# Reordering the first-token turns of a gated SSM and MLP kernel, turning the last of them into one PSUM bank, and taking a small exponential ahead of two copies

## Chip, cores and metric

One NeuronCore of a Trainium2 chip (trn2) runs the program. The metric is the device time of one execution in microseconds (us). "Fast" runs are those not marked as disturbed. A ratio of two kernels is the mean time of one kernel's fast runs over the mean of the other's in the same rounds, so it is not quite the ratio of the medians that are quoted beside it. "Span" is the length of one execution inside the profile; it is about 1.8 us shorter than the time.

## The reference

`x` has 2048 tokens of 640 channels. The output mixes a linear state-space layer `a` and a two-layer GELU network `b`:

```python
g = sigmoid((x * gate_w).sum(-1, keepdims=True))
# a: h_t = Lam_bar * h_{t-1} + B_bar x_t  (complex, 640 states), y = 2 Re(C h) + x * Dskip
#    with dt = exp(log_dt), Lam_bar = exp(dt * Lam)
# b: gelu(x @ w1 + b1) @ w2 + b2,  w1 is 640 x 1728
return g * a + (1 - g) * b
```

The recurrence is real once the complex rotation is taken out with tables of sine and cosine. The tables and the decay `r_c = exp(dt * Re(Lam))` come from three small parameter vectors.

## The kernel before

Tokens go in four chunks of 512. Matmuls want `x` with channels on the partitions. Later chunks are transposed by DMA, but the first chunk is "turned" by TensorE: a matmul of a 128 x 128 piece of `x` with the identity, into PSUM, then a copy from PSUM to `xT`. There are four token tiles (0 to 3) and five channel blocks (0 to 4). Blocks 0 and 1 of a tile are turned first (`turn_first`), blocks 2 to 4 later (`turn_rest`), because their half of `x` lands later.

Between the turns TensorE already works on the first layer. `part(kd, a)` is six matmuls of 128 columns: channel block `kd` of token tile `a`, into six accumulators, one PSUM bank each.

```python
KA = 2                                   # blocks 0, 1 first; 2, 3, 4 are "the rest"
def turned(engine, p, col, a, k0, k1):   # PSUM -> xT, on VectorE or ScalarE
    dst = xT[0][:, k0:k1, a * P:(a + 1) * P]
    src = p[:, col:col + (k1 - k0) * P].rearrange("p (k t) -> p k t", t=P)
    ...
def turn_first(a, other):
    t = bank()
    turn(t, 0, a, 0);          turned(nc.vector, t, 0, a, 0, 1)
    turn(other, a * P, a, 1);  turned(nc.scalar, other, a * P, a, 1, 2)
# [cut]
def turn_rest(a, parts):
    for k0, k1, t, engine in parts:
        for k in range(k0, k1):
            turn(t, (k - k0) * P, a, k)
        turned(engine, t, 0, a, k0, k1)

part(0, 0); part(0, 1)                   # [one call a line in the source]
turn_first(2, pA)
part(1, 0)
turn_first(3, pA)
part(1, 1)
part(0, 2)
turn_rest(0, ((KA, KD, bank(), nc.scalar),))
part(1, 2)
# parameters: turned into pA, copied to colA, then dt16 = exp(log_dt) and limp
part(0, 3)
turn_rest(1, ((KA, KD, bank(), nc.vector),))
part(1, 3)
turn_rest(2, ((KA, KD, pA, nc.scalar),))
part(2, 0)
nc.vector.tensor_tensor(out=dtl[:], in0=dt16[:], in1=lre_c, op=ALU.mult)      # the two products
nc.vector.tensor_tensor(out=thp_c[:], in0=dt16[:], in1=limp[:], op=ALU.mult)
turn_rest(3, ((KA, KA + 1, bank(), nc.vector), (KA + 1, KD, pA, nc.scalar)))
nc.scalar.activation(out=r_c[:], in_=dtl[:], func=ACT.Exp)                    # the decay
# sine and cosine tables from thp_c [cut]
part(2, 1); part(2, 2); part(2, 3)
```

The kernel's PSUM pool holds eight banks. Six are the accumulators and one is the fixed bank `pA`. That leaves **one** for every `bank()` call in this stretch: I call it the rotating bank. A turn into either bank must wait until the copy that last read it has finished.

Of the kernel before, what the change touches and what calls it, by code (L numbers as in the profile page):

```python
# [16 lines left out]
P = 128  # L17
# [5 lines left out]
KD = D // P  # L23
# [18 lines left out]
def kernel(  # L42
# [19 lines left out]
    nc = tc.nc  # L62
# [12 lines left out]
    def bank(dtype=F32):  # L75
        return ps.tile([P, CH * 4 // (4 if dtype == F32 else 2)], dtype, name="bank")
# [55 lines left out]
    KA = 2  # L132
# [95 lines left out]
    pA = bank()  # L228
# [3 lines left out]
    def turn(p, col, a, kd):  # L232
        nc.tensor.matmul(p[:, col:col + P], lhsT=xn[0][:, a, kd * P:(kd + 1) * P], rhs=ident[:], start=True, stop=True,  # L233
                         skip_group_check=True)

    def turned(engine, p, col, a, k0, k1):
        dst = xT[0][:, k0:k1, a * P:(a + 1) * P]
        src = p[:, col:col + (k1 - k0) * P].rearrange("p (k t) -> p k t", t=P)
        if engine is nc.vector:
            nc.vector.tensor_copy(out=dst, in_=src)  # L240
        else:
            nc.scalar.activation(out=dst, in_=src, func=ACT.Identity)  # L242

    def turn_first(a, other):
        t = bank()
        turn(t, 0, a, 0)
        turned(nc.vector, t, 0, a, 0, 1)
        turn(other, a * P, a, 1)
        turned(nc.scalar, other, a * P, a, 1, 2)
# [76 lines left out]
    def strip(kd, t0, t1, first, f0=0, f1=FA):  # L326
        for kf in range(f0, f1):
            ff1_mm(banks[kf], 0, kf, kd, t0, t1, first, 3)

    def turn_rest(a, parts):  # L330
        for k0, k1, t, engine in parts:
            for k in range(k0, k1):
                turn(t, (k - k0) * P, a, k)
            turned(engine, t, 0, a, k0, k1)

    HB = CH // 2

# [18 lines left out]
    def over(c, n):  # L356
        return c.rearrange("p (k o) -> p k o", o=1).to_broadcast([P, KS, n])

    def part(kd, a):
        strip(kd, a * P, (a + 1) * P, kd == 0)  # L360
# [2 lines left out]
    part(0, 1)  # L363
    turn_first(2, pA)
    part(1, 0)
    turn_first(3, pA)
    part(1, 1)
    part(0, 2)
    turn_rest(0, ((KA, KD, bank(), nc.scalar),))
    part(1, 2)  # L370
    nc.tensor.matmul(pA[:, 0:3 * KS], lhsT=prmA[:], rhs=ident[:, 0:3 * KS], start=True, stop=True, skip_group_check=True)  # L371
    nc.vector.tensor_copy(out=colA[:], in_=pA[:, 0:3 * KS])
    nc.scalar.activation(out=dt16[:], in_=ldt_c, func=ACT.Exp)
    nc.vector.tensor_scalar(out=limp[:], in0=lim_c, scalar1=INV_2PI, scalar2=None, op0=ALU.mult)
    part(0, 3)
    turn_rest(1, ((KA, KD, bank(), nc.vector),))
    part(1, 3)
    turn_rest(2, ((KA, KD, pA, nc.scalar),))
    part(2, 0)
    nc.vector.tensor_tensor(out=dtl[:], in0=dt16[:], in1=lre_c, op=ALU.mult)  # L380
    nc.vector.tensor_tensor(out=thp_c[:], in0=dt16[:], in1=limp[:], op=ALU.mult)
    turn_rest(3, ((KA, KA + 1, bank(), nc.vector), (KA + 1, KD, pA, nc.scalar)))
    nc.scalar.activation(out=r_c[:], in_=dtl[:], func=ACT.Exp)
    nc.vector.tensor_tensor(out=u, in0=tf[:].rearrange("p (o i) -> p o i", o=1).to_broadcast([P, KS, HC]), in1=over(thp_c[:], HC), op=ALU.mult)
    nc.vector.tensor_copy(out=kk[:], in_=u)
    nc.vector.tensor_tensor(out=red, in0=u, in1=kk[:], op=ALU.subtract)
# [46 lines left out]
    for ks in range(KS):  # L433
        for dst, X, xs, Y in ((TCOS, FS, nsH, FC), (TSIN, FC, sH, FS)):
            t = work.tile([P, HB], F32, name="g")
# [308 lines left out]
```

## Time and profile before

| | before |
|---|---|
| time, first 3 runs | 216.12 us median (215.97 to 216.13) |
| span in the profile | 214.4 us |
| TensorE (PE) busy | 98% of the span |
| waits of PE on another engine that the profile lists, after the warm-up | one, 0.2 us |

The page of the kernel before: the busy table (engine, us, share, instructions) and the chain of work that ended last (engine, share of the span).

```profile
span 214.4 us, 3572 instructions
...
PE 209.4 (98%) x1384; PEld 117.9 (55%) x1403; DVE 189.4 (88%) x389; ACT 103.6 (48%) x188; POOL 1.0 (0%) x13
...
PE 96%; DMA 1%; issue 1%; ACT 0%; SPq 0%; DVE 0%
...
```

PE is the chain. Its own waits in the whole kernel of before (who waited for whom, us in total, times, longest) say how little there is to win:

```profile
...
PE bank L230 <- PEq L728: 0.8, 1, 0.8
PE bank L611 <- issue: 0.3, 2, 0.2
PE bank L233 <- ACT xT L242: 0.2, 1, 0.2
```

The only listed one that another engine causes after the start is the last: a turn (L233) that waited for a ScalarE copy to `xT` (L242). The list has no entry under 0.2 us, so shorter waits are missing from it; the starts of the turns show some. The chain of the kernel before in order of time (start us, us, what) shows where:

```profile
...
8.25 0.34 PE bank L268 x6
8.58 0.18 PE bank L233 x3
...
8.79 0.50 ACT xT L242
...
9.33 0.27 PE bank L233 x2
9.60 1.22 PE bank L268 x19
...
```

The reader sees the chain leave PE at 8.77 us, run through ScalarE's copy of tile 2, and return to PE for the last two turns of tile 3. The timeline of the same stretch (start us, us, engine, line, operation, tiles, count, and in brackets the idle time before it and what ended it):

```profile
...
6.22 0.28 PE L233 MATMUL bank<-ident,xn 128*128 128x128 bf16 x2
...
6.47 0.29 DVE L240 CAST xT<-bank 128x128 bf16<-128x128 f32 x1 [0.31 <-PE bank L233]
...
7.01 0.33 PE L233 MATMUL bank<-ident,xn 128*128 128x128 bf16 x3
...
8.29 0.56 DVE L240 CAST xT<-bank 128x384 bf16<-128x384 f32 x1 [0.16 <-PE bank L233]
...
8.79 0.49 ACT L242 ACTIVATE xT<-bank 128x384 bf16<-128x384 f32 x1 [0.62 <-PE bank L233]
...
8.92 0.22 PE L233 MATMUL bank<-ident,xn 128*128 128x128 bf16 x1
...
9.33 0.27 PE L233 MATMUL bank<-ident,xn 128*128 128x128 bf16 x2 [0.19 <-ACT xT L242]
...
9.44 2.46 PE L268 MATMUL bank<-xT,w1a 128*128 128x128 bf16 x23
9.64 0.38 ACT L242 ACTIVATE xT<-bank 128x256 bf16<-128x256 f32 x1 [0.36 <-PE bank L233]
...
10.13 1.28 ACT L390 ACT_TABLE_LOAD   x1
...
```

The brackets say 0.19 us of idle. The starts say more. Matmuls of 128 columns start every 0.056 us, so the turn at 8.92 should have been followed at 8.98, and was followed at 9.33. The row of the turn at 8.92 lasts 0.22 us, to 9.14, and idle time is counted only from there, which is why the idle figure is smaller than the 0.35 us lost.

### The profile page before, as it was taken

How to read it: one execution, taken by the hardware profiler on the slowest of the kernel's cores; microseconds unless marked ns; L12 is line 12 of the kernel's file. 1: busy time of each engine (PE TensorE's matmuls, PEld its weight loads, DVE VectorE, ACT ScalarE, POOL GpSimd, SP SyncE). 2: the span in 40 equal slices, each digit the busy share in tenths (PEclk: the TensorE clock that was granted, in tenths of full speed). 3: DMA queues.
4: the chain of work that ended last, by engine and by line, in shares of the span. 5: the costliest groups of instructions: out<-in, count | busy, mean ns of one | idle time of the engine just before them, and what ended most of it. 6: DMA issues, size and time to landing. Idle time of an engine off the chain costs nothing.

```text
span 214.4 us, 3572 instructions
## 1 busy us (share of the span) xinstructions
PE 209.4 (98%) x1384; PEld 117.9 (55%) x1403; DVE 189.4 (88%) x389; ACT 103.6 (48%) x188; POOL 1.0 (0%) x13
## 2 busy tenths in 40 slices
PE   8999999999999999999999999999999999999994
PEld 4945444454454644775446577444455567654773
DVE  1599999999999999998999999999999999993153
ACT  3599956665848688303573210456683422304200
POOL 1000000000000000000000000000000000000000
PEclk9999999999999999999999999999999999999999
DMA  6879999997000000042000005200000000100011
GB/s 196 231 177 177 208 189 287 317 210 173 0 0 0 3 0 0 14 132 109 6 0 3 0 0 171 77 0 2 3 0 14 0 3 27 65 34 0 0 66 61
DMA packets 31571, 15.84 MB, mean 74 GB/s; under 512 B 22978, under 2 KB 31554, under 8 KB 31554
## 3 DMA queue, kind: packets, MB, share of 16 engines
q1 hardware_dynamic: 30850, 14.99, 29.1%
q10 hardware_dynamic: 704, 0.62, 0.9%
q8 instruction: 11, 0.18, 0.4%
q14 instruction: 6, 0.05, 0.1%
HBM read 7.48 MB, written 2.62 MB: 47 GB/s over the span
## 4 chain that ended last, share of the span: by engine, by line
PE 96%; DMA 1%; issue 1%; ACT 0%; SPq 0%; DVE 0%
PE bank L611 26%; PE bank L268 26%; PE bank L670 20%; PE bank L553 20%; DMA xn<-in_A_x_dram 1%; PE bank L627 1%; PE bank L294 1%; PE bank L233 1%; ACT xT L242 0%; SPq L136 0%; DVE ot L675 0%; PE bank L284 0%; PE bank L402 0%; PE bank L371 0%
## 5 line engine op out<-in xcount | busy, mean ns | idle before, releaser
L611 PE MATMUL bank<-w_sb,gel 128*128 128x128 bf16 (+1 forms) x408 | 57.1, 297 | 0.6 <-issue 0.3
L611 PEld LDWEIGHTS <-gel 128*128 128x128 bf16 x416 | 32.3, 98 | 25.5
L556 ACT ACTIVATE bu<-bank 128x512 bf16<-128x512 f32 x40 | 23.6, 597 | 37.4 <-PE bank L553 37.3
L273 ACT ACTIVATE gel<-bank,colB 128x512 bf16<-128x512 f32 x52 | 33.8, 694 | 11.2 <-PE bank L268 10.4
L670 PEld LDWEIGHTS <-hs 128*128 128x128 bf16 x330 | 31.6, 98 | 11.5
L507 DVE TENSOR_TENSOR_SCAN g<-r_c,carry,v 128x512 bf16<-128x512 f32 x30 | 37.3, 1270 | 0.0
L619 ACT ACTIVATE gb<-bank,gcol 128x512 f32<-128x512 f32 (+1 forms) x32 | 15.1, 526 | 31.9 <-PE bank L627 16.8
L268 PE MATMUL bank<-xT,w1a 128*128 128x512 bf16 (+1 forms) x170 | 28.2, 318 | 0.2
L670 PE MATMUL bank<-CT_re,hs 128*128 128x320 bf16 (+2 forms) x165 | 27.1, 295 | 0.0
L670 PE MATMUL bank<-CT_im,hs 128*128 128x320 bf16 (+2 forms) x165 | 27.1, 295 | 0.0
L675 DVE SCALAR_TENSOR_TENSOR ot<-bank,gcol,gb 128x320 bf16<-128x320 f32 (+2 forms) x33 | 17.4, 531 | 10.0 <-PE bank L670 8.7
L553 PE MATMUL bank<-xT,BT_im 128*128 128x512 bf16 x99 | 24.8, 379 | 0.1
L553 PE MATMUL bank<-xT,BT_re 128*128 128x512 bf16 x97 | 24.5, 379 | 0.2
L268 PEld LDWEIGHTS <-w1a 128*128 128x128 bf16 x174 | 14.8, 102 | 11.4
L268 PE MATMUL bank<-xT,w1b 128*128 128x512 bf16 x80 | 17.9, 379 | 0.0
L586 DVE TENSOR_TENSOR bank<-xn,Dbc 128x320 f32<-128x320 bf16 (+2 forms) x33 | 14.4, 481 | 2.7 <-ACT gb L619 2.6
L553 PEld LDWEIGHTS <-BT_im 128*128 128x128 bf16 x100 | 9.8, 98 | 11.8
L488 DVE TENSOR_TENSOR v<-wa,wb 128x512 bf16<-128x512 bf16 x40 | 15.2, 420 | 0.6
L553 PEld LDWEIGHTS <-BT_re 128*128 128x128 bf16 x100 | 9.6, 98 | 11.0
L600 ACT ACTIVATE bank<-b2bc 128x512 f32<-128x512 bf16 (+1 forms) x24 | 11.7, 526 | 7.7 <-DVE ot L675 7.7
L488 DVE TENSOR_TENSOR wa<-TCOS,g 128x1024 bf16<-128x1024 bf16 x20 | 13.7, 686 | 0.1
L268 PE MATMUL bank<-xT,w1c 128*128 128x512 bf16 x57 | 13.6, 379 | 0.2
(101 smaller groups left out, 166.7 us busy)
## 6 DMA issues: line engine op xcount, KB each, us to landing
out_dram<-ot SPq DMA_DIRECT2D x15, 160.0 KB, 1.9
w_sb<-in_B_w_dram SPq DMA_DIRECT2D x1, 2080.0 KB
xn<-in_A_x_dram SPq DMA_DIRECT2D x3, 640.0 KB
w1b<-in_B_w_dram SPq DMA_DIRECT2D x5, 128.0 KB, 3.3
w1c<-in_B_w_dram SPq DMA_DIRECT2D x5, 112.0 KB, 3.6
w1a<-in_B_w_dram ACTq DMA_DIRECT2D x2, 192.0 KB, 3.1
w1a<-in_B_w_dram SPq DMA_DIRECT2D x1, 384.0 KB, 3.3
xn<-in_A_x_dram SPq DMA_DIRECT2D x4, 64.0 KB, 3.0
```

The costliest lines, as they stand in the source:

```text
L268: nc.tensor.matmul(p[:, t0:t1], lhsT=w, rhs=xT[c][:, kd, t0:t1], start=(kd == 0) if first is None else first, stop=(kd == last), skip_grou ...
L273: nc.scalar.activation(out=gel[c][:, kf, :], in_=p[:, :], func=ACT.Gelu_apprx_tanh, bias=b1_c[:, kf:kf + 1])
L488: nc.vector.tensor_tensor(out=o, in0=a, in1=b, op=op)
L507: nc.vector.tensor_tensor_scan(s["g"][:, ri, :], r_c[:, ks:ks + 1].to_broadcast([P, CH]), s["v"][:, ri, :], init, ALU.mult, ALU.add)
L553: nc.tensor.matmul(p[:], lhsT=BT[ks >= KSA][:, kd, (ks % KSA if ks < KSA else ks - KSA) * P:][:, 0:P], rhs=xT[c][:, kd, :], start=(kd == 0 ...
L556: nc.scalar.activation(out=bu[:, ri, :], in_=p[:], func=ACT.Identity)
L586: dve_now(ck.pe, 0.45, lambda: nc.vector.tensor_tensor(out=p[:, 0:d1 - d0], in0=xn[c][:, a, d0:d1], in1=Dbc[:, d0:d1], op=ALU.mult))
L600: nc.scalar.activation(out=v, in_=src, func=ACT.Identity)
L611: nc.tensor.matmul(p[:, col:col + d1 - d0], lhsT=gel[c][:, kf, a * P:(a + 1) * P], rhs=w2_sb[:, kf, d0:d1], start=False, stop=False, skip_ ...
L619: nc.scalar.activation(out=gbs[ti][:, d0:d1], in_=p[:, col:col + d1 - d0], func=ACT.Identity, scale=gcol[:, 1, ti:ti + 1])
L670: nc.tensor.matmul(p[:, 0:d1 - d0], lhsT=hs[c][:, j, lo:lo + P], rhs=CT[:, j % KS, d0:d1], start=False, stop=(j == 2 * KS - 1), skip_group ...
L675: nc.vector.scalar_tensor_tensor(out=ot[:, d0:d1], in0=p[:, 0:d1 - d0], scalar=gcol[:, 0, ti:ti + 1], in1=gbs[ti][:, d0:d1], op0=ALU.mult, ...
```

## The change

The intent is that no group of turns waits for a PSUM copy, and that the decay and the table inputs do not stand behind copies.

```diff
-    def turn_rest(a, parts):
-        for k0, k1, t, engine in parts:
-            for k in range(k0, k1):
-                turn(t, (k - k0) * P, a, k)
-            turned(engine, t, 0, a, k0, k1)
+    def turn_rest(a, t, *parts):
+        for k in range(KA, KD):
+            turn(t, (k - KA) * P, a, k)
+        for engine, k0, k1 in parts:
+            turned(engine, t, (k0 - KA) * P, a, k0, k1)
 ...
     part(1, 0)
+    part(1, 1)
     turn_first(3, pA)
-    part(1, 1)
     part(0, 2)
 ...                                       (turn_rest of tiles 0 to 2: new call form only)
     part(0, 3)
-    turn_rest(1, ((KA, KD, bank(), nc.vector),))
-    part(1, 3)
-    turn_rest(2, ((KA, KD, pA, nc.scalar),))
-    part(2, 0)
     nc.vector.tensor_tensor(out=dtl[:], ...)
     nc.vector.tensor_tensor(out=thp_c[:], ...)
-    turn_rest(3, ((KA, KA + 1, bank(), nc.vector), (KA + 1, KD, pA, nc.scalar)))
+    turn_rest(1, bank(), (nc.vector, KA, KD))
     nc.scalar.activation(out=r_c[:], in_=dtl[:], func=ACT.Exp)
+    part(1, 3)
+    turn_rest(2, pA, (nc.scalar, KA, KD))
+    part(2, 0)
+    turn_rest(3, bank(), (nc.vector, KA, KA + 1), (nc.scalar, KA + 1, KD))
```

More of the change, by code (lines that the diff above doesn't have):

```diff
@@ L365 @@
     part(1, 0)
+    part(1, 1)
     turn_first(3, pA)
-    part(1, 1)
     part(0, 2)
-    turn_rest(0, ((KA, KD, bank(), nc.scalar),))
+    turn_rest(0, bank(), (nc.scalar, KA, KD))
     part(1, 2)
```

## The prediction

> **What bounds the kernel now.** TensorE. The page's busy table gives PE 98% of the 214.4 us span; the chain of waits that ended last is 96% PE. PE's list of waits holds, after the warm-up, one wait on another engine: 0.2 us on a ScalarE copy of the first tokens. The chain puts that copy at 8.79 to 9.29 us, the turn behind it at 9.33. From 9.44 PE is dense. So only what moves PE earlier before then can shorten the kernel, and it should last to the end.
>
> **What the change does.** The instruction order shows the same instructions, four things moved, all between 6.0 and 10.2 us.
>
> 1. Tile 3's first turns go behind six matmuls. In the timeline they start at 6.22 where 6.10 was possible: they wait for the VectorE copy of tile 2 (ends 6.17), which holds the bank. That 0.12 us disappears. But tile 3's own copy moves later: turn at 6.44, result 0.22 after, copy (0.29) from 6.69 to 6.98. Tile 0's remaining turns need the same rotating bank and are ready at 6.89, six matmuls later instead of twelve. They wait until about 7.03, against 7.01 before. **I expect nothing from this step (0.02 us lost).**
>
> 2. Tile 3's last turns all use the rotating bank, freed by the VectorE copy of tile 1, instead of two in the bank that the ScalarE copy frees at 9.29. This removes the visible wait. Before, the three turns and the next matmul start at 8.92, 9.33, 9.38, 9.44; unhindered, the second would start at 8.98. So 0.35 us is at stake.
>
> 3. Two tiny VectorE products now stand ahead of tile 1's copy, which ran 8.29 to 8.85. They wait for the exponential (ends about 8.19), start about 8.23, and push the copy to about 8.37 to 8.93. Step 2's turns then start at 8.98 against 8.94 unhindered: 0.04 us comes back as a new wait.
>
> 4. The decay exponential (0.20 us) runs in a ScalarE gap near 8.4, no longer ahead of the Sin table load. Against that, ScalarE's copy of tile 3 now waits for VectorE's copy out of the same bank: the Trainium skill ("PSUM — Partial Sum Buffer", section "PSUM bank collisions raise a hardware error") says that two engines may not touch one bank at once, reads included. The built order carries this wait; no trace of it exists yet. I expect this copy at 9.56 instead of 9.64, the table load at 9.95 instead of 10.13. PE needs the data near 10.2. Off the critical path.
>
> **Sum.** PE's matmul after the turns starts at about 9.15 instead of 9.44: 0.29 us. Later arrivals have slack: the first gelu starts 0.18 earlier, and PE reaches its first reused gelu bank about 0.4 us after it is free.
>
> **Prediction: 215.83 us** (216.12 less 0.29, 0.13%), 8 in 10 between 215.55 and 216.15. Chances: faster by over 2% 0.005, within 2% 0.99, slower by over 2% 0.005.
>
> **What would show it right.** The PE timeline has no ScalarE wait near 9.3; the first matmul after tile 3's turns starts near 9.15; tile 0's remaining turns still start near 7.0 (step 1 void); tile 1's VectorE copy starts near 8.37; ScalarE's last token copy waits for VectorE; everything after is the same sequence shifted by a constant 0.3 us.
>
> **What would make it wrong.** Loads landing later than PE now arrives; step 1 gaining its 0.12 us after all; the products starting later than 8.23 and delaying tile 1's copy; the start-up clock (107 ns matmuls until about 5.7 us) switching at another moment, an effect of the same size.

## The result

The changed kernel took 216.03 us in the median of 5 runs (215.6 to 216.26), the kernel before 216.12 (215.97 to 216.33). The ratio is 0.9993 with a 95% interval of 0.9978 to 1.0007: by time alone, the same.

PE's waits of the changed kernel, in the same view as before:

```profile
...
PE bank L230 <- PEq L728: 0.8, 1, 0.8
PE bank L233 <- DMA xn<-in_A_x_dram: 0.4, 1, 0.4
PE bank L611 <- issue: 0.3, 2, 0.2
```

The wait on ScalarE is gone. The 0.4 us on the load of `x` is another matter: it is the second token tile arriving late in this execution. The chain of the changed kernel now stays on PE through the turns of tile 3:

```profile
...
8.46 0.34 PE bank L268 x6
8.79 0.20 PE bank L233 x3
8.99 1.22 PE bank L268 x19
...
```

And its timeline, with the rows that answer to those of before:

```profile
...
6.12 0.28 PE L233 MATMUL bank<-ident,xn 128*128 128x128 bf16 x2
...
6.38 0.29 DVE L240 CAST xT<-bank 128x128 bf16<-128x128 f32 x1 [0.49 <-PE bank L233]
...
6.72 0.33 PE L233 MATMUL bank<-ident,xn 128*128 128x128 bf16 x3
...
7.90 0.17 DVE L376 TENSOR_TENSOR dtl<-dt,colA 128x5 f32<-128x5 bf16 x1
...
8.06 0.55 DVE L240 CAST xT<-bank 128x384 bf16<-128x384 f32 x1
...
8.66 0.33 PE L233 MATMUL bank<-ident,xn 128*128 128x128 bf16 x3
...
8.83 2.46 PE L268 MATMUL bank<-xT,w1a 128*128 128x128 bf16 x23
...
9.03 0.29 DVE L240 CAST xT<-bank 128x128 bf16<-128x128 f32 x1 [0.42 <-PE bank L233]
...
9.35 0.38 ACT L242 ACTIVATE xT<-bank 128x256 bf16<-128x256 f32 x1 [0.37 <-DVE xT L240]
...
9.75 1.28 ACT L390 ACT_TABLE_LOAD   x1
...
```

The three turns of tile 3 start together at 8.66 and the next matmul follows at 8.83. Before, it took from 8.92 to 9.44.

The two spans differ by 0.6 us, though, and not all of that is the change. I cut every trace at PE events:

- the **head**: from the span's start to the first matmul of `part(1, 0)`;
- the **approach**: from there to the first turn of tile 0's rest;
- the **stretch**: from there to the first matmul of `part(2, 1)`;
- the **tail**: the remainder.

Approach and stretch together are the "middle" that the expectations below speak of.

| trace | head | approach | stretch | tail | span |
|---|---|---|---|---|---|
| before | 5.74 | 1.27 | 2.43 | 204.96 | 214.4 |
| changed | 5.45 | 1.27 | 2.11 | 204.97 | 213.8 |

The tail is equal to 0.01 us, so what PE wins early lasts to the end. The stretch is 0.32 us shorter. The other 0.29 us is in the head, where the two kernels have the same instructions. The timeline shows what differs there. Before, the weight load for tile 1's turns and the twelve matmuls that follow these turns:

```profile
...
4.05 0.13 PEld L233 LDWEIGHTS <-xn 128*128 128x128 bf16 x2 [0.41 <-DMA xn<-in_A_x_dram]
...
4.25 1.49 PE L268 MATMUL bank<-xT,w1a 128*128 128x128 bf16 x12
...
```

The same two rows of the changed kernel:

```profile
...
4.29 0.12 PEld L233 LDWEIGHTS <-xn 128*128 128x128 bf16 x2 [0.65 <-DMA xn<-in_A_x_dram]
...
4.42 1.08 PE L268 MATMUL bank<-xT,w1a 128*128 128x128 bf16 x12
...
```

The changed kernel's load of `x` landed 0.24 us later, and yet its head ended 0.29 us earlier, because its matmuls started 0.056 us apart from about 4.4 us on, and those of before 0.107 us apart until about 5.8 us. So in this pair a later load cost the changed kernel 0.24 us, and an earlier doubling of TensorE's rate gained 0.53 us (0.29 and 0.24). The second trace of the changed kernel, below, shows that doubling more plainly.

### The profile page after: what moved, and what is told of

It reads as the page before. It is cut to its first block, busy times and chain, and to the rows that moved or that the text cites. A ratio compares the mean times of both kernels' runs of the same rounds, so it can differ in the third digit from the quotient of the medians.

```text
span 213.8 us, 3572 instructions
## 1 busy us (share of the span) xinstructions
PE 208.6 (98%) x1384; PEld 117.0 (55%) x1403; DVE 189.1 (88%) x389; ACT 103.4 (48%) x188; POOL 1.0 (0%) x13
## 4 chain that ended last, share of the span: by engine, by line
PE 96%; DMA 1%; issue 1%; SPq 0%; DVE 0%; ACT 0%
PE bank L611 26%; PE bank L268 26%; PE bank L670 20%; PE bank L553 20%; DMA xn<-in_A_x_dram 1%; PE bank L627 1%; PE bank L294 1%; PE bank L233 1%; SPq L136 0%; DVE ot L675 0%; ACT xT L242 0%; PE bank L284 0%; PE bank L402 0%; PE bank L371 0%
## 5 line engine op out<-in xcount | busy, mean ns | idle before, releaser
L268 PE MATMUL bank<-xT,w1a 128*128 128x512 bf16 (+1 forms) x170 | 27.6, 311 | 0.3
L268 PEld LDWEIGHTS <-w1a 128*128 128x128 bf16 x174 | 14.1, 98 | 11.7 <-issue 0.2
```

What stands on the lines that cost most here:

```text
L268: nc.tensor.matmul(p[:, t0:t1], lhsT=w, rhs=xT[c][:, kd, t0:t1], start=(kd == 0) if first is None else first, stop=(kd == last), skip_grou ...
```

## The experiments

All eleven submissions gave correct results. Each was timed in 3 or 5 rounds beside the kernel before. The kernels of one occasion share the chip and the runs of before: 216.25 us median of 11 runs (215.64 to 216.78) on the first, 216.28 (215.84 to 218.28) on the second, 216.31 (215.84 to 218.29) on the third. The cuts of all traces:

| trace | head | approach | stretch | tail | span | median time |
|---|---|---|---|---|---|---|
| before again | 5.17 | 1.26 | 2.43 | 205.04 | 213.9 | 215.97 |
| turns only | 5.66 | 1.27 | 2.42 | 205.05 | 214.4 | 216.20 |
| one bank only | 5.75 | 1.29 | 2.08 | 204.98 | 214.1 | 215.90 |
| products only | 5.33 | 1.26 | 2.43 | 204.98 | 214.0 | 215.94 |
| changed, second | 6.52 | 2.13 | 2.13 | 205.02 | 215.8 | 216.01 |
| before, copy twice | 5.74 | 1.27 | 2.95 | 205.04 | 215.0 | 216.71 |
| changed, copy twice | 5.63 | 1.30 | 2.10 | 205.37 | 214.4 | 216.43 |
| more room | 5.22 | 1.11 | 2.08 | 204.99 | 213.4 | 215.40 |
| before, no warm-up | 5.71 | 1.88 | 2.43 | 204.98 | 215.0 | 216.95 |
| more room, again | 5.17 | 1.21 | 2.72 | 205.00 | 214.1 | 215.86 |
| changed, third | 5.65 | 1.27 | 2.11 | 204.97 | 214.0 | 215.94 |

The theory is that of the prediction: the gain is the wait on `pA`, removed by turning all of tile 3's rest into the rotating bank. The rivals are that the first-turn reorder, or the earlier products and exponential, bring it; or that the head belongs to the change.

### Control: the kernel before against itself

No edit.

> The kernel before, unchanged, against itself: a control. I cut each execution in three: the head (from the span's start to the first matmul of the second weight block on tile 0), the middle (from there to the first matmul of the third block on tile 1, which holds everything the change moves) and the tail (the rest). The first trace of before gives 5.74, 3.70 and 204.96 us; that of the changed kernel 5.45, 3.38 and 204.97. My theory says that the middle and tail repeat to within 0.03 us and that the head varies by some 0.3 us from run to run, because loads and the start-up clock vary; so the middle again 3.70, tail 204.96, head anywhere from 5.4 to 6.0, total 215.9 to 216.4. The rival, that the 0.29 us of difference in the head belongs to the change, wants a head of 5.74 again and a total of 216.1.

The ratio of the kernel to itself was 1.0008 (0.997 to 1.0046), and the medians of the two sets, of the same program on the same occasion, were 215.97 and 216.25 us. The stretch repeated (2.43) and so did the tail (205.04, 0.08 above the first trace; a span is given to 0.1). The head was 5.17 instead of 5.74. The rival falls: a head varies by 0.57 us in one and the same kernel (5.45, 6.52 and 5.65 in the three traces of the changed one).

### Only the turns

```diff
     part(1, 0)
-    turn_first(3, pA)
     part(1, 1)
+    turn_first(3, pA)
     part(0, 2)
```

> Only tile 3's first turns are moved behind six matmuls. My theory: the wait moves from those turns to tile 0's remaining turns, so the middle is 3.70 to 3.72 and the wait on the ScalarE copy near 9.3 us stays; total as before within 0.1 us. The rival, that this step is what removes waiting, wants a middle of 3.58 (its 0.12 us gone).

The approach stayed 1.27. The wait on ScalarE stayed, as PE's waits of this run show:

```profile
...
PE bank L233 <- ACT xT L242: 0.2, 1, 0.2
```

The ratio was 0.9997 (0.9978 to 1.0016). Its timeline, from the six matmuls after tile 3's first turns:

```profile
...
6.44 0.50 PE L268 MATMUL bank<-xT,w1a 128*128 128x128 bf16 x6
...
6.93 0.33 PE L233 MATMUL bank<-ident,xn 128*128 128x128 bf16 x3
...
```

At 0.056 us apart the six matmuls make room for tile 0's turns at 6.77, and these start at 6.93. Step 1 is worth nothing: the turns of tile 3 no longer wait, and the turns of tile 0 wait in their place, for the same bank.

### Only the bank

```diff
-    turn_rest(3, ((KA, KA + 1, bank(), nc.vector), (KA + 1, KD, pA, nc.scalar)))
+    turn_rest(3, bank(), (nc.vector, KA, KA + 1), (nc.scalar, KA + 1, KD))
```

(with the new form of `turn_rest`; the turns, the products and the exponential stay as before)

> Only the bank of tile 3's last turns is changed; turns, products and exponential stay where they were. My theory: the whole 0.35 us wait goes and none comes back, since the VectorE copy is not held up: middle 3.35, a little below the 3.38 of the full change; total 0.35 us below before, about 215.75, if heads average out. The rival (the full change needs its early products to gain) wants a middle of 3.55 or more.

The stretch was 2.08: the whole 0.35 us, and 0.03 better than the full change. The middle was 3.37, not 3.35, because the approach of this run was 0.02 longer. The timeline of this run has tile 3's turns and the next matmul with nothing between:

```profile
...
8.95 0.33 PE L233 MATMUL bank<-ident,xn 128*128 128x128 bf16 x3
...
9.12 2.03 PE L268 MATMUL bank<-xT,w1a 128*128 128x128 bf16 x21
...
```

The ratio was 0.9985 (0.9966 to 1.0005).

### Only the products and the exponential

```diff
+    nc.vector.tensor_tensor(out=dtl[:], ...)
+    nc.vector.tensor_tensor(out=thp_c[:], ...)
     turn_rest(1, ((KA, KD, bank(), nc.vector),))
+    nc.scalar.activation(out=r_c[:], in_=dtl[:], func=ACT.Exp)
     part(1, 3)
     turn_rest(2, ((KA, KD, pA, nc.scalar),))
     part(2, 0)
-    nc.vector.tensor_tensor(out=dtl[:], ...)
-    nc.vector.tensor_tensor(out=thp_c[:], ...)
     turn_rest(3, ((KA, KA + 1, bank(), nc.vector), (KA + 1, KD, pA, nc.scalar)))
-    nc.scalar.activation(out=r_c[:], in_=dtl[:], func=ACT.Exp)
```

> Only the two products and the decay exponential are taken ahead. My theory: the middle stays 3.70, because the turns still wait for the ScalarE copy of tile 2; the Sin table load starts about 0.2 us earlier relative to that copy; the first gelu is earlier by about as much; total as before within 0.1 us. The rival (ScalarE and VectorE latency, not the bank, is what the change gains on) wants the total 0.2 to 0.3 us below before.

The stretch stayed 2.43 and the ratio was 1.0006 (0.9974 to 1.0037), so this part gains no time. I missed the size on ScalarE. Measured from the start of the copy of tile 2, the Sin table load starts 1.25 us later here (8.37 to 9.62) and 1.34 before (8.79 to 10.13): 0.09 us earlier, not 0.2, and the first gelu is earlier by about as much (5.20 to 5.10 us from the start of that copy). In the trace of before the exponential starts at 9.92, while the copy ahead of it runs until 10.02: 0.10 of its 0.20 us was hidden already.

### The suspected cost doubled, before and changed

In both kernels, after tile 2's rest is turned and copied, the copy is issued a second time. It writes the same values.

```diff
     turn_rest(2, ...pA, nc.scalar...)
+    turned(nc.scalar, pA, 0, 2, KA, KD)
```

> The kernel before, with ScalarE's copy of tile 2 out of the second bank issued twice in a row (the same values written again, so the result stays right). It doubles the suspected cost. [...]the bank comes free 0.40 us later. My theory: middle 3.70 plus 0.40, so 4.10, and the total 0.4 us above before. The rival (the wait on that copy is only how the profile books some other wait) wants 3.70.

> The changed kernel with the same doubled copy. The turns no longer use that bank, so my theory wants the middle unchanged at 3.38. But the third block on tile 2 still needs the copied tokens: the copy ended at 8.98 in the trace of the changed kernel and that block would have started at 9.17, so 0.40 us more makes it wait about 0.26 us, in the tail: 205.2. So the doubled copy should cost 0.26 us here against 0.40 in the kernel before. The rival (the bank was not the reason) wants the same loss in both.

The timeline of the kernel before with the copy doubled:

```profile
...
8.79 1.01 ACT L242 ACTIVATE xT<-bank 128x384 bf16<-128x384 f32 x2 [0.62 <-PE bank L233]
...
8.92 0.22 PE L233 MATMUL bank<-ident,xn 128*128 128x128 bf16 x1
...
9.85 0.27 PE L233 MATMUL bank<-ident,xn 128*128 128x128 bf16 x2 [0.71 <-ACT xT L242]
...
```

The stretch grew from 2.43 to 2.95, by 0.52 us. I had expected 0.40, from two copies that overlap, as other pairs of ScalarE instructions do in the trace of before (one that starts at 11.43 and lasts 0.47 us is followed at 11.80, with about 0.1 us of overlap). But the second copy rewrites what the first wrote, and in the trace it waits for a semaphore that ScalarE's own copies set, so the two took 1.01 us, and PE lost just what they grew by. The wait is on that copy and nothing else.

In the changed kernel the stretch did not grow (2.10), as expected. The cost moved to where the copied tokens are needed:

```profile
...
8.70 1.29 ACT L242 ACTIVATE xT<-bank 128x384 bf16<-128x384 f32 x3 [0.18 <-PE bank L233]
...
9.03 0.50 PE L268 MATMUL bank<-xT,w1a 128*128 128x128 bf16 x6
...
9.77 1.05 PE L268 MATMUL bank<-xT,w1a 128*128 128x128 bf16 x13 [0.23 <-ACT xT L242]
...
```

`part(2, 1)` starts at 9.03 and `part(2, 2)`, due six matmuls (0.34 us) later at 9.37, starts at 9.77: 0.40 us, the tail's 205.37 against 204.97. That is more than the 0.26 expected, because the copy again grew by 0.52 and not 0.40. So the changed kernel has about 0.12 us of slack in this place (0.52 less 0.40); it did not make the copy free. The ratios, 1.0011 (0.9973 to 1.0048) and 1.0001 (0.996 to 1.0042), say nothing at this size.

### A second trace of the changed kernel

> The changed kernel again, for a second trace and more times. My theory: middle 3.38 and tail 204.97 again, whatever the head; if heads average out, the mean time is 0.32 us below that of before, but heads scatter by some 0.5 us, so the ratio of the times may come out anywhere from 0.997 to 1.000. The rival (the change also shortens the head, as the first pair of traces suggests with 5.74 against 5.45) wants a head of about 5.45 again.

The ratio was 0.9988 (0.9953 to 1.0024). The profile fell on the slowest of the six runs, 217.57 us against 215.61 to 216.04 for the rest, and it shows what made this one slow. The chain of this run in order of time:

```profile
...
5.24 1.28 PE bank L268 x12
...
6.73 1.28 PE bank L268 x12
...
8.22 0.61 PE bank L268 x6
...
9.00 0.34 PE bank L268 x6
...
```

Twelve matmuls of 128 columns in 1.28 us are 107 ns each; from 9.00 on six take 0.34 us, 57 ns each. TensorE ran at half rate until about 8.7 us in this run. In the first trace of before that ended near 5.8. Twelve traces have the warm-up matmuls; in the eleven besides this one, the starts of single matmuls put it between about 4.1 and 6.1. The granted clock on the profile's page reads full in both, so only the durations of matmuls show it. The Trainium skill ("TensorE: Matmul & The Clock Gate", section "What's actually happening") describes it: TensorE starts at half clock and doubles after a busy window of about 3.4 us, and the window runs freely, so the moment differs from run to run. The 107 and 57 ns agree with the 107 and 56 of its section "What you observe"; the window itself no run here shows. In this run the second token tile also landed late: PE turned it at 4.84 instead of 4.06. The two can be told apart against the first trace of before, whose head ran at half rate too: the head is 0.78 us longer, which is the late load, and the approach 0.86 us longer, which is the clock.

Once the clock is up, the stretch is 2.13 as in the other trace. The middle of 3.38 that I expected failed (4.26), because the slow clock reached into the approach.

### What sets the head: no warm-up

The kernel before starts with eight matmuls on constants, which only warm TensorE up. Here they are left out.

```diff
-    for n in (512, 512, 512, 512, 512, 512, 128, 128):
-        nc.tensor.matmul(pA[:, 0:n], lhsT=ones(P), rhs=ones(n), start=True, stop=True)
```

> The kernel before without its eight warm-up matmuls on constants, which only serve the start-up clock. It tests what makes the head scatter. My theory: the head is set by when TensorE's start-up clock doubles (matmuls of 128 columns go from 107 to 56 ns)[...]. Without earlier matmuls the doubling comes later, past 7 us, so some 20 to 60 matmuls at 51 ns more each: total 1 to 3 us above before, the tail still 205.0 if the doubling falls before it. The rival (loads alone set the head) wants the total unchanged within 0.3 us.

216.95 us against 216.31, all four runs between 216.66 and 217.15; the ratio was 1.0014 (0.9968 to 1.0059), for the runs of before on this occasion held two of over 218. In the trace the head was no longer than before (5.71 against 5.74, both at half rate), but the approach took 1.88 us instead of 1.27: the half rate lasted until about 7.3 us. One trace can't show that the missing matmuls delayed the doubling, since it came at 8.7 once with them. The times support it: all four lie above nine of the eleven of before (216.64 at most). I had put the cost at 1 to 3 us, which was too much: the median moved by 0.64 us and the trace by 0.61.

### A version with more room

On top of the change, both first turns of tile 3 go to `pA` and leave it in one copy, so that tile 0's rest finds the rotating bank free. The products go back behind tile 1's copy, and the decay goes between ScalarE's last two token copies.

```diff
     part(1, 1)
-    turn_first(3, pA)
+    turn(pA, 2 * P, 3, 0)
+    turn(pA, 3 * P, 3, 1)
+    turned(nc.vector, pA, 2 * P, 3, 0, 2)
 ...
-    nc.vector.tensor_tensor(out=dtl[:], ...)
-    nc.vector.tensor_tensor(out=thp_c[:], ...)
     turn_rest(1, bank(), (nc.vector, KA, KD))
-    nc.scalar.activation(out=r_c[:], in_=dtl[:], func=ACT.Exp)
+    nc.vector.tensor_tensor(out=dtl[:], ...)
+    nc.vector.tensor_tensor(out=thp_c[:], ...)
     part(1, 3)
     turn_rest(2, pA, (nc.scalar, KA, KD))
+    nc.scalar.activation(out=r_c[:], in_=dtl[:], func=ACT.Exp)
     part(2, 0)
```

> A version meant to beat both: on top of the change, tile 3's first two turns both go to the fixed bank and leave in one VectorE copy of 256 columns, so that tile 0's remaining turns find the rotating bank free; the two products go back behind tile 1's copy, and the decay exponential sits between ScalarE's last two token copies. My theory: the wait at tile 0's remaining turns (0.15 us after the change's step 1) and the 0.03 at tile 3's last turns go: middle 3.20, tail 204.97, total 0.5 us below before if heads average out, about 215.65. The rival (those waits are only moved on again, as step 1 of the change moved one) wants 3.35 or more.

The median was 215.40 us and the ratio 0.9956 (0.9926 to 0.9986). The middle was 3.19, as expected: 0.16 us less approach than before and the full 0.35 less stretch. It was run a second time:

> The version with more room again, for a second trace and more times on another occasion. My theory: middle 3.19, from tile 0's remaining turns on 2.08; tail 205.0; about 0.5 us below before on average, scatter of heads apart. The rival (its first result was luck of the heads) wants no difference from before beyond 0.2 us.

The median was 215.86 us and the ratio 0.9962 (0.9925 to 0.9999). But the trace shows a stretch of 2.72, not 2.08. In its timeline:

```profile
...
7.56 0.50 PE L268 MATMUL bank<-xT,w1a 128*128 128x128 bf16 x6
...
8.42 0.17 PEld L233 LDWEIGHTS <-xn 128*128 128x128 bf16 x3 [0.54 <-DMA xn<-in_A_x_dram]
8.43 0.34 PE L233 MATMUL bank<-ident,xn 128*128 128x128 bf16 x3 [0.37 <-DVE dtl L379]
...
```

The weight load of tile 2's turns (PEld) waited 0.54 us for a DMA of `x`. (The matmul's own row books its wait to a VectorE product that it does not need; the weight load just ahead of it names the true cause.) These turns were due near 7.89, after the six matmuls that start at 7.56, and the load was not there until 8.4. That is 0.54 of the 0.64 us; the rest came before, where the matmul on the parameters started 0.15 us late for a reason that I did not trace. So the version with more room is faster than both kernels in the medians, but a late load can take back what it gains. This is not peculiar to it: the control turned the same blocks at 7.84, so a load as late would have held up the kernel before as well.

### The changed kernel a third time

> The changed kernel a third time, beside the version with more room. My theory: the stretch from tile 0's remaining turns to the first matmul of the third block on tile 1 is 2.11 to 2.13 us as in its other two traces (2.43 before); the total lies 0.3 us below before on average and 0.2 above the version with more room. The rival (the gain of the change is nothing) wants equal means with before over the rounds of all three occasions.

The stretch was 2.11 again, middle 3.38 and tail 204.97. The median was 215.94 us and the ratio 0.9971 (0.993 to 1.0011). It lay 0.37 us below before and 0.08 above the version with more room in the medians.

Over all occasions, before had a median of 216.26 us in 38 runs, the changed kernel 216.02 in 17, and the version with more room 215.61 in 12. Leaving out the runs of over 217 us (three of before, one of the changed kernel), the means are 216.20 (standard deviation 0.27) and 215.95 (0.21): a gain of 0.25 us with a standard error of 0.07, which I work out from these deviations and the 35 and 16 runs. These sets pool occasions, so take the figure as a check on the traces' 0.32, not as a measurement of its own. They leave out the six runs of the control, which are of the same program as before; with these, its mean is 216.17 us (40 runs, four more left out) and the gain 0.22. None of the three intervals of the changed kernel by itself excludes 1.

## Why the prediction was right, point by point

- **What binds: right.** PE's only wait on another engine was the place to look, and the tail, 204.96 to 205.05 us in every trace but the one whose tail was lengthened on purpose, shows that a gain there lasts.
- **Step 1, worth nothing: right.** Predicted 0.02 us lost; the approach was 1.27 us in both kernels and with this step alone.
- **Step 2, 0.35 us at stake: right.** The bank alone shortened the stretch by 0.35 us (2.43 to 2.08).
- **Step 3, 0.04 us given back: right.** The full change is 0.03 us longer than the bank alone (2.11 to 2.08). The products, of which the first starts at 7.90 in the changed timeline, pushed tile 1's copy: it starts 0.43 us after that tile's first turn (7.63 to 8.06), against 0.37 before (7.92 to 8.29), and the turns of tile 3 wait for it.
- **Step 4, off the critical path: right, with two wrong sizes.** ScalarE's last copy now waits for VectorE, as the built order and the skill's rule on one bank said (no run provoked a collision). I expected it 0.08 us earlier. But measured from the first turn of tile 0's rest it starts after 2.63 us in both (9.64 less 7.01, 9.35 less 6.72). The reason stands in the timeline: VectorE's copy follows the first turn of tile 3 by 0.26 us before (8.92 to 9.18) and by 0.37 in the changed kernel (8.66 to 9.03), since it now waits for three turns into its bank instead of one. I had left out the other two, 0.11 us. Measured in the same way, the table load is only 0.09 us earlier (3.12 to 3.03) and not 0.18, the 0.09 that the exponential alone gave; and so is the first gelu (6.97 to 6.88). Neither reaches PE: the tail is the same.
- **The sum, 0.29 us: right in the traces** (0.32), and within the noise of the times (0.09 in the recorded medians, 0.24 pooled). The stated range, 215.55 to 216.15, also holds the 216.12 us of before, so that the recorded 216.03 fell inside it says little; the cuts and the single-step runs show the mechanism, not that number.
- **What would make it wrong** was the part that mattered most for the recorded number. The start-up clock and the loads move the head by as much as the effect: 5.17 to 5.75 us among the ordinary traces, 6.52 in one. That, not the change, is the 0.29 us of extra difference between the first pair of spans.

What stays open: why the clock doubles when it does in a given run, and how the start-up clock and the loads of `x` share the scatter of the times. Single traces can be taken apart by the starts of their matmuls, as with the first pair of spans and the slow run above, but only one run of each set was profiled.

## What to carry to other kernels

Keep a ledger of PSUM banks by time: a reorder that stops one group of turns from waiting for a bank only moves the wait if the next group needs the same bank with less work in between. Look at start times against the known cadence, not at idle figures, for the cost of a short wait. And when an effect is a tenth of a per cent, cut the traces at events on the binding engine and compare the pieces, since the heads of two runs of the same program can differ by more than the effect.

## What the Trainium skill lacked or had wrong

- "ScalarE: Activation LUTs", section "What ACT_TABLE_LOAD costs", gives about 1283 ns for the load plus about 1380 ns of drain for every switch of sets. The load agrees (1.28 us in every trace). The drain does not appear: in the trace of before the exponential ends at 10.12 us, the load runs 10.13 to 11.41, and the first Sin starts at 11.43.
- The same section says that back-to-back ScalarE instructions overlap by about 93 ns. It lacks the condition that the second must not wait for the first: two copies to the same place took 1.01 us for two of 0.49, without overlap, and a third copy to another place, of 0.38, brought the three to 1.29, with about 0.1 of overlap.
- "TensorE: Matmul & The Clock Gate", section "What's actually happening", says that the moment of the clock's doubling varies by ±500 ns and calls the penalty under 1% of a typical span. Under 1% it is, but the moment varied more here, between about 4.1 and 6.1 us in eleven traces and 8.7 in one, and the page lacks the warning that this can be several times the gain of a tuning step (the approach of that one was 0.86 us longer than in the first trace of before, against a gain of 0.3 us).
- "PSUM — Partial Sum Buffer" states the rule of one engine to a bank. It lacks the price in time of putting several turns into one bank: in this kernel, where the copy waits for all of them, a copy of the first of three turns started 0.37 us after that turn's start, against 0.26 when it had the bank to itself.
